# Bias of the last spatial sum on VectorE, one mask for all heads, and a new order table

## The chip, the cores and the metric

The kernel runs on one core of a Trainium2 chip. The metric is the device time of one execution in microseconds (us), the median over several runs. The engines are named as the profile names them: PE (TensorE matmuls, PEld its weight loads), DVE (VectorE), ACT (ScalarE), POOL (GpSimd) and SP (SyncE, which issues nearly all DMAs).

## The reference

Two layers stand one behind the other. The first is a gated recurrence over 768 steps for 4 batches and 8 heads of width 48; the second is a feed-forward block with a spatial sum over the sequence. Inputs and output are float32.

```python
# first layer, for each batch and head (D = 48), t = 0 .. 767
state = alpha[t, :, None] * state + outer(k[t], v[t])      # 48 x 48
y[t]  = q[t] @ state
# second layer: x is y with the heads side by side, [4, 768, 384]
h   = relu(x @ w_in)                                       # 384 -> 1024
u, v = h[..., :512], h[..., 512:]
v_n = (v - mean(v)) / sqrt(var(v) + 1e-6)                  # over the 512
v_s = einsum('ts,bsd->btd', w_spatial, v_n) + b_spatial[None, :, None]
out = (u * v_s) @ w_out                                    # 512 -> 384
```

## The kernel before

The sequence is cut into chunks of 128 steps, 6 for each batch and 24 in all. In a chunk the recurrence becomes matrix products: cumulated sums of log(alpha) (`cum`), keys and queries scaled by their exponentials (`kt`, `qt`), their transposes (`tr`, `trk`), scores (`sc`), a causal mask on the scores (`m`), and the output `y` from the masked scores and from the state of the chunk before. The first eight chunks are done in pairs with even and odd steps apart (`pair`, lines 368 to 584), the other sixteen one by one (`first`, lines 586 to 742).

The mask is a multiplication on DVE of a PSUM bank of scores (128 x 512: four heads of 128) with a bf16 tile of zeros and ones. The tiles are built once at the start: `mask4` (line 166, four equal triangles side by side, for single chunks, read on line 717) by POOL in `c_m4`, and `mask2` (line 184, for pairs, one set of four equal triangles for each of two parities, read on line 546) by two memsets on DVE (line 1031) and four selections on POOL (`c_m2`, line 230; the selections show as line 196).

In the second layer each batch has six groups of x @ w_in for v (`v`) and eight for u (`u`), eight spatial sums (`s`, one for each of four slices of 128 features and each half of the sequence), and six output tiles (`o`; the last tile of the last batch goes in two halves, `oh`). A spatial sum is six matmuls into one bank (line 780). For 31 of the 32 sums DVE then adds the bias `bsp_bc` into a float32 buffer `vsb` (line 928), and a second instruction on POOL or DVE multiplies with `uT` into `gT` (`g`, line 941). For the 32nd (`last`, line 907) the bias is put into the bank by a matmul of `ident` with `bsp_bc` ahead of the six, and one DVE instruction multiplies bank and `uT` into `gT` (line 921).

No scheduler runs on the chip or in the compiler. Each step is an `Op` with the engines that may do it; `replay` (line 62) walks through a table `PLAN` (line 58) that was worked out ahead, whose words give the engine and the number of a step. So the table sets the order on each engine, and for steps with a choice also the engine. Each engine works through its instructions in that order and waits at each for what it needs. PSUM has eight banks, taken in turn in the order in which the table starts steps. A word of the table can carry numbers behind colons: for each, `bank` (line 126) puts one float32 matmul on a constant tile `junk` of so many columns ahead of the step on PE (line 138). Nothing reads what these fillers make; they occupy PE near the start. One filler shows as two matmul records in the profile.

Of the kernel before, what the change touches and what calls it, by code (L numbers as in the profile page):

```python
# [9 lines left out]
FP32 = mybir.dt.float32  # L10
# [64 lines left out]
def kernel(  # L75
# [76 lines left out]
    def copy_pairs(eng, out, in_):  # L152

        copy(eng, *((out.bitcast(FP32), in_.bitcast(FP32)) if eng == "ACT" else (out, in_)))

    def relu(eng, out, in_):
        if eng == "ACT":
            nc.scalar.activation(out=out, in_=in_, func=AF.Relu)  # L158
        else:
            ENG[eng].tensor_scalar_max(out=out, in0=in_, scalar1=0.0)  # L160
# [24 lines left out]
    sbd_bufs = [consts.tile([128, HP, 2 * D], BF16, name=f"sbd{i}") for i in range(NB)]  # L185

    def zero_padding(t):

        flat = t.bitcast(FP32)
        nc.vector.memset(flat[:, :, :, D // 2:32], 0.0)  # L190
        if t.shape[2] > H:
            nc.vector.memset(flat[:, :, 0::3, 0:D // 2], 0.0)

    def triangle(t, pattern, base=0, step=1):

        nc.gpsimd.affine_select(
            out=t, in_=t, compare_op=ALU.is_gt, fill=1.0, base=base, channel_multiplier=step, pattern=pattern)
# [170 lines left out]
    def pair(j):  # L368
# [158 lines left out]
        for par in range(2):  # L527
            def sc(_, par=par):
                for s in range(2):
                    st[f"pt{s}{par}"] = bank([128, HP, 128])  # L530
                for hp in range(HP):
                    for s in range(2):
                        for ci in range(2):
                            rows = slice(64 - 64 * s, 64 - 64 * s + D)
                            nc.tensor.matmul(  # L535
                                out=st[f"pt{s}{par}"][halves(ci), hp, :], lhsT=st["kT"][rows, par, hp, halves(ci)],
                                rhs=q_cols(rows, hp, ci), start=True, stop=True)

            sls = [Slot(ring), Slot(ring)]
            op(("sc", j, par), "PE", 0.41, sc, got(("ev", "k", j, par), ("ev", "q", j, 0), ("ev", "q", j, 1)),  # L540
               prio=P + 7, take=sls, cols=768)
            for s in range(2):
                def mk(_, par=par, s=s):
                    if f"ptm{par}" not in st:
                        st[f"ptm{par}"] = work.tile([128, 2, HP, 128], BF16, name="ptm", bufs=4)
                    nc.vector.tensor_tensor(  # L546
                        out=st[f"ptm{par}"][:, s], in0=st[f"pt{s}{par}"], in1=mask2[:, par], op=ALU.mult)

                op(("m", j, par, s), "DVE", 0.6, mk,
                   got(("sc", j, par), ("y", 2 * j - 4), ("y", 2 * j - 3), ("c_m2", par)), prio=P + 7.5, use=[sls[s]])  # L550
# [35 lines left out]
    def first(i):  # L586
# [126 lines left out]
        def mk(s):  # L713
            def emit(_):
                if "ptm" not in st:
                    st["ptm"] = work.tile([128, 2, HP, 128], BF16, name="ptm", bufs=4)
                nc.vector.tensor_tensor(out=st["ptm"][:, s], in0=st[f"pt{s}"], in1=mask4, op=ALU.mult)  # L717
            return emit

        for s, sl in ((0, sl0), (1, sl1)):  # L720
            op(("m", i, s), "DVE", 0.6, mk(s), got(("sc", i), ("y", i - WK), ("c_m4",)), prio=P + 7.5, use=[sl])
# [184 lines left out]
    def second_s(b, dsl, th):  # L906
        last = b == B - 1 and dsl == NDS - 1 and th == 1
        mms = []
        if last:
            mms.append(mm(  # L910
                lambda ps: ps[:, 0:TH], lambda: ident, lambda: bsp_bc[:, th, :], True, False))
        for st in range(NT):
            mms.append(mm(
                lambda ps: ps[:, 0:TH].rearrange("p (c t) -> p c t", c=3), lambda st=st: bt[b]["vn"][:, st, dsl * 128:(dsl + 1) * 128],
                lambda st=st: w_spT[:, 3 * th:3 * th + 3, st, :], st == 0 and not last, st == NT - 1))
        hold = {}
        cols = slice(th * TH, (th + 1) * TH)

        def evac(eng, ps):
# [207 lines left out]
```

## Time and profile before

| what | value |
|---|---|
| median of 3 runs | 139.5 us (139.48 to 140.99) |
| the profiled execution | 139.22 us |
| its span, first to last instruction | 137.4 us |
| granted TensorE clock, mean | 0.995 |
| POOL busy | 92.9 us (68% of the span) |
| DMA | 28.64 MB, mean 208 GB/s |

The span is 1.8 us shorter than the time of the same execution. Rows of the profile that group instructions give, behind the bar, their busy time in us and the mean duration of one in ns, and behind a second bar the idle time of the engine just before them. Rows of the timeline and of the chain begin with the start in us from the span's start and the length in us; xN says how many instructions are merged in a row.

### The profile page before, as it was taken

The numbers are of one execution on the slowest core, as the hardware profiler recorded it, in microseconds if no ns is written. First come the engines' busy times: TensorE is split into PE (matmuls) and PEld (weight loads), VectorE is DVE, ScalarE is ACT, GpSimd is POOL, SyncE is SP. The second block draws the span as 40 slices with busy tenths as digits, with TensorE's granted clock in tenths as the row PEclk, the third lists the DMA queues.
The fourth block names the chain that finished last, engine by engine and source line by source line (L and its number), as shares of the span: only waits on it lengthen the run. The fifth ranks groups of instructions, "written<-read, shape, count | busy, mean of one in ns | idle before, by whom it ended". The sixth has DMA issues, their size and how long they took to land.

```text
span 137.4 us, 5023 instructions
## 1 busy us (share of the span) xinstructions
PE 132.7 (97%) x1943; PEld 88.4 (64%) x1943; DVE 116.1 (84%) x278; ACT 101.3 (74%) x286; POOL 92.9 (68%) x165
## 2 busy tenths in 40 slices
PE   6999999999999999999999999999999999999990
PEld 6768885757667655775667665656666666555660
DVE  7157989998998979998899999989999989878640
ACT  3488687999874799989974887999966757760241
POOL 4734998899894898793399999825666785202910
PEclk9999999999999999999999999999999999999998
DMA  3999999998979899899998989999994602940355
GB/s 95 319 322 328 275 343 328 331 293 243 319 120 314 160 193 203 166 208 193 207 210 160 212 168 199 196 200 212 193 183 114 169 10 108 350 171 6 130 188 197
DMA packets 89000, 28.64 MB, mean 208 GB/s; under 512 B 83728, under 2 KB 87440, under 8 KB 88976
## 3 DMA queue, kind: packets, MB, share of 16 engines
q1 hardware_dynamic: 88800, 28.22, 83.8%
q8 instruction: 15, 0.25, 0.7%
q10 hardware_dynamic: 144, 0.10, 0.2%
q14 instruction: 9, 0.07, 0.1%
q0 software_dynamic: 32, 0.00, 0.0%
HBM read 23.60 MB, written 4.72 MB: 206 GB/s over the span
## 4 chain that ended last, share of the span: by engine, by line
PE 95%; ACT 1%; issue 1%; DVE 0%; ACTq 0%
PE bank L780 58%; PE bank L138 7%; PE bank L671 3%; PE bank L706 3%; PE bank L470 3%; PE bank L734 2%; PE bank L618 2%; PE bank L692 2%; PE bank L535 2%; PE bank L728 2%; PE bank L406 2%; PE bank L343 2%; PE bank L505 2%; PE bank L562 1%; PE bank L320 1%; PE bank L792 1%
## 5 line engine op out<-in xcount | busy, mean ns | idle before, releaser
L780 PE MATMUL bank<-w_spT,vn 128*128 128x384 bf16 x192 | 35.1, 326 | 0.0
L941 POOL TENSOR_TENSOR gT<-vsb,uT 128x384 bf16<-128x384 f32 x25 | 22.8, 928 | 9.2 <-DVE vsb L928 8.6
L780 PEld LDWEIGHTS <-vn 128*128 128x128 bf16 x192 | 17.5, 97 | 10.5
L717 DVE TENSOR_TENSOR ptm<-bank,mask 128x512 bf16<-128x512 f32 x32 | 20.6, 681 | 0.1
L642 POOL TENSOR_TENSOR kt<-kc,binv 128x384 bf16<-128x384 f32 x15 | 13.9, 932 | 9.6 <-ACT binv L630 5.4
L780 PE MATMUL bank<-xT,w_in 128*128 128x384 bf16 x96 | 19.4, 326 | 0.0
L780 PE MATMUL bank<-w_in,xT 128*128 128x512 bf16 x72 | 19.2, 379 | 0.0
L928 DVE TENSOR_TENSOR vsb<-bank,bsp_bc 128x384 f32<-128x384 f32 x31 | 16.6, 552 | 2.0 <-PE bank L780 1.6
L780 PE MATMUL bank<-w_out_sb,gT 128*128 128x384 bf16 (+1 forms) x100 | 18.2, 319 | 0.0
L158 ACT ACTIVATE uT<-bank 128x384 bf16<-128x384 f32 x25 | 11.9, 495 | 5.5 <-PE bank L780 5.5
L150 POOL CAST sbd<-state 64x192 bf16<-64x192 f32 x40 | 13.7, 344 | 2.6 <-DVE state L290 0.5
L845 DVE BATCH_NORM_STATS2 stats<-v_sb 128x6 f32<-128x512 bf16 x20 | 13.7, 686 | 0.2
L148 ACT COPY kqT<-bank 128x256 f32<-128x256 f32 x35 | 11.8, 387 | 2.6 <-PE bank L671 1.7
L158 ACT ACTIVATE v_sb<-bank 128x512 bf16<-128x512 f32 x18 | 10.8, 598 | 3.1 <-PE bank L780 2.6
L290 POOL TENSOR_TENSOR state<-state,bc 128x192 f32<-128x192 f32 x17 | 9.5, 559 | 4.9 <-DVE state L283 2.6
L780 PEld LDWEIGHTS <-w_in 128*128 128x128 bf16 x96 | 8.7, 97 | 6.1
L138 PE MATMUL bank<-junk 128*128 128x64 f32 (+5 forms) x44 | 11.4, 389 | 1.1 <-DVE junk L1012 1.1
L780 PEld LDWEIGHTS <-gT 128*128 128x128 bf16 x100 | 8.9, 97 | 5.4 <-POOL gT L941 0.4
L148 ACT CAST x_sb<-bank 128x384 bf16<-128x384 f32 x20 | 9.4, 490 | 3.3 <-PE bank L734 2.3
L546 DVE TENSOR_TENSOR ptm<-bank,mask 128x512 bf16<-128x512 f32 x16 | 10.0, 682 | 0.5 <-PE bank L535 0.5
L612 ACT ACTIVATE la<-ac 128x384 bf16<-128x384 f32 x16 | 8.4, 533 | 2.5 <-DMA ac<-in_alpha_dram 2.5
L138 PEld LDWEIGHTS bank<-junk 128*128 128x128 f32 x44 | 8.8, 242 | 2.0 <-DVE junk L1012 1.1
(133 smaller groups left out, 290.7 us busy)
## 6 DMA issues: line engine op xcount, KB each, us to landing
ac<-in_alpha_dram SPq DMA_DIRECT2D x16, 192.0 KB, 4.6
kc<-in_k_dram SPq DMA_DIRECT2D x16, 192.0 KB, 4.0
qc<-in_q_dram SPq DMA_DIRECT2D x16, 192.0 KB, 3.9
vc<-in_v_dram SPq DMA_DIRECT2D x16, 192.0 KB, 3.9
raw_w<-in_moe_w_spatial_dram SPq DMA_DIRECT2D x3, 768.0 KB, 4.7
out_dram<-raw_w SPq DMA_DIRECT2D x11, 192.0 KB, 2.0
out_dram<-o_sb SPq DMA_DIRECT2D x9, 192.0 KB, 1.9
ac<-in_alpha_dram SPq DMA_DIRECT2D x4, 384.0 KB, 4.6
```

The source lines that it names most:

```text
L138: nc.tensor.matmul(out=flat[:, 0:cols].rearrange("p (a b) -> p a b", a=4), lhsT=junk, rhs=junk[:, None, 0:n].to_broadcast([128, 4, n]), st ...
L148: nc.scalar.copy(out=out, in_=in_)
L150: ENG[eng].tensor_copy(out=out, in_=in_)
L158: nc.scalar.activation(out=out, in_=in_, func=AF.Relu)
L290: ENG[eng].tensor_tensor(out=st["state"], in0=st["state"], in1=st["bc"][:, :, None].to_broadcast([128, HP, D]), op=ALU.mult)
L546: nc.vector.tensor_tensor(out=st[f"ptm{par}"][:, s], in0=st[f"pt{s}{par}"], in1=mask2[:, par], op=ALU.mult)
L642: ENG[eng].tensor_mul(out=k_blocks(kt3)[:, :, :, 0:D], in0=quad(st["kc"]), in1=st["binv"])
L717: nc.vector.tensor_tensor(out=st["ptm"][:, s], in0=st[f"pt{s}"], in1=mask4, op=ALU.mult)
L780: return lambda ps: nc.tensor.matmul(out=out(ps), lhsT=lhsT(), rhs=rhs(), start=start, stop=stop)
L845: nc.vector.bn_stats(out=stats, in_=d["v_sb"][:, tt, :])
L928: nc.vector.tensor_tensor(out=hold["vs"], in0=ps[:, 0:TH], in1=bsp_bc[:, th, :], op=ALU.add)
L941: ENG[eng].tensor_tensor(out=bt[b]["gT"][:, dsl, cols], in0=hold["vs"], in1=bt[b]["uT"][:, dsl, cols], op=ALU.mult)
```

## The change

Three things are changed. The 32nd spatial sum is treated as the 31 others are: the matmul with `ident` is gone, a bias addition and a separate multiplication come in place of the one multiplication. The masks hold one triangle (`ut_ones`, which was there already, in place of `mask4`) or one for each parity (`mask2`), and are read with a repeat over the heads; `mask4` and its step are gone, and `mask2` is built by one memset on DVE and two selections on POOL. And the table is a new one, since steps are numbered anew: nearly every engine's order is different, some steps go to another engine, and the fillers are others.

```diff
 PLAN = """
-S110 Q111 D0 D17 D5 G47 Q48 D3 D6 D1 S49 Q50 D11 D2 D15 S53 Q54 D13 D12 G14 D4 A118 S51 Q52 G16 A57 S55 Q56 P119:192:64:128:192:320:192:192:64 G9 P58
...
+S107 Q108 D2 D6 D0 D3 D1 D10 S46 Q47 D4 D14 D5 G15 D11 S48 Q49 D12 D7 G13 A115 S52 Q53 G8 P116:192:128:512:128:64 A54
...
-    mask4 = consts.tile([128, 4, 128], BF16, name="mask4")
...
-    mask2 = consts.tile([128, 2, 4, 128], BF16, name="mask2")
+    mask2 = consts.tile([128, 2, 128], BF16, name="mask2")
...
-    def c_m4(_):
-        nc.gpsimd.memset(mask4.bitcast(FP32), 0.0)
-        triangle(mask4, [[0, 4], [-1, 128]])
+    def of_heads(mask):
+
+        return mask[:, None, :].to_broadcast([128, HP, 128])
...
-    def c_m2(par):
-
-        def emit(_):
-            for ci in range(2):
-                triangle(mask2[64 * ci:64 * ci + 64, par], [[0, 4], [-1, 2], [-2, 64]], par, 2)
-        return emit
+    def c_m2(_):
+        for ci in range(2):
+            triangle(mask2[64 * ci:64 * ci + 64], [[1, 2], [-1, 2], [-2, 64]], 0, 2)
...
-                        out=st[f"ptm{par}"][:, s], in0=st[f"pt{s}{par}"], in1=mask2[:, par], op=ALU.mult)
+                        out=st[f"ptm{par}"][:, s], in0=st[f"pt{s}{par}"], in1=of_heads(mask2[:, par]), op=ALU.mult)
...
-                nc.vector.tensor_tensor(out=st["ptm"][:, s], in0=st[f"pt{s}"], in1=mask4, op=ALU.mult)
+                nc.vector.tensor_tensor(out=st["ptm"][:, s], in0=st[f"pt{s}"], in1=of_heads(ut_ones), op=ALU.mult)
...
     def second_s(b, dsl, th):
-        last = b == B - 1 and dsl == NDS - 1 and th == 1
+        last = False
...
-    op(("c_m4",), "POOL", 0.95, c_m4, prio=-8.0 if PAIRS else -18.0)
...
-        for par in range(2):
-            op(("c_mz", par), "DVE", 0.25, lambda _, par=par: nc.vector.memset(mask2[:, par].bitcast(FP32), 0.0), prio=-18.2)
-            op(("c_m2", par), "POOL", 1.4, c_m2(par), got(("c_mz", par)), prio=-18.0 + par)
+        op(("c_mz",), "DVE", 0.12, lambda _: nc.vector.memset(mask2.bitcast(FP32), 0.0), prio=-18.2)
+        op(("c_m2",), "POOL", 0.75, c_m2, got(("c_mz",)), prio=-18.0)
```

Three places show what the new table moves. The first is PE at the start of the program: the fillers (line 138 before, 188 after, matmuls of `junk`) and the first cumulated sums (line 406 before, 452 after). Before:

```order
L138 MATMUL bank0_85<-junk_97 128x192
L138 MATMUL bank0_85<-junk_97 128x64
L138 MATMUL bank0_85<-junk_97 128x128
L138 MATMUL bank0_85<-junk_97 128x192
L138 MATMUL bank0_85<-junk_97 128x320
L138 MATMUL bank0_85<-junk_97 128x192 x2
L138 MATMUL bank0_85<-junk_97 128x64
L406 LDWEIGHTS le_pair_116
L406 MATMUL bank0_85<-la1_108,le_pair_116 128x384
```

The same place after:

```order
L188 MATMUL bank0_85<-junk_96 128x192
L188 MATMUL bank0_85<-junk_96 128x128
L188 MATMUL bank0_85<-junk_96 128x512
L188 MATMUL bank0_85<-junk_96 128x128
L188 MATMUL bank0_85<-junk_96 128x64
L452 LDWEIGHTS le_pair_115
L452 MATMUL bank0_85<-la1_107,le_pair_115 128x384
```

Ahead of the first sum there are 1344 columns of fillers before and 1024 after. Over the whole program it is 3200 columns in 22 fillers before and 2368 in 15 after; all of them stand in the first quarter of PE's steps.

The second place is POOL near the start, where the masks were built (line 196 before; line 245 after, ahead of this piece), between the identity's copy and the products for the keys (`kt`, lines 442 and 488). Before:

```order
L1020 COPY ident_q_95<-ident_94 128x2x64
L203 MEMSET ut_ones_93 128x128
L196 AFFINE_SELECT ut_ones_93<-ut_ones_93 128x128
L442 TENSOR_TENSOR kt0_111<-kc_163,binvp1_114 128x4x2x48
L290 TENSOR_TENSOR state_303<-state_303,bc2_246 128x192
L196 AFFINE_SELECT mask2_118<-mask2_118 64x512 x2
L442 TENSOR_TENSOR kt1_112<-kc_203,binvp0_113 128x4x2x48
L150 CAST vbp_400<-vc_249 128x384
```

The same place after:

```order
L1066 COPY ident_q_95<-ident_94 128x2x64
L488 TENSOR_TENSOR kt1_111<-kc_211,binvp2_114 128x4x2x48
L488 TENSOR_TENSOR kt1_111<-kc_211,binvp0_112 128x4x2x48
L200 CAST sbd0_118<-state_284 64x4x48 x2
L336 TENSOR_TENSOR state_320<-state_320,bc2_217 128x192
L200 CAST vbp_397<-vc_269 128x384 x2
```

The two selections that stood ahead of the second pair's keys are gone from there, and POOL makes both of that pair's keys, where before DVE made one.

The third place is DVE at the end of the program: the last bias additions (`vsb`), multiplications (`gT`) and copies of output tiles (`raw_w`, `o_sb`). Before:

```order
L928 TENSOR_TENSOR vsb0_122<-bank3_88,bsp_bc_105 128x384
L928 TENSOR_TENSOR vsb1_123<-bank0_85,bsp_bc_105 128x384
L928 TENSOR_TENSOR vsb2_124<-bank2_87,bsp_bc_105 128x384
L921 TENSOR_TENSOR gT_2568<-bank3_88,uT_2565 128x384
L150 COPY raw_w_3143<-bank5_90 128x384
L150 COPY o_sb_3162<-bank0_85 128x384
```

The same place after:

```order
L974 TENSOR_TENSOR vsb1_122<-bank2_87,bsp_bc_104 128x384
L987 TENSOR_TENSOR gT_2567<-vsb0_121,uT_2564 128x384
L974 TENSOR_TENSOR vsb2_123<-bank1_86,bsp_bc_104 128x384
L974 TENSOR_TENSOR vsb3_124<-bank3_88,bsp_bc_104 128x384
L987 TENSOR_TENSOR gT_2567<-vsb3_124,uT_2564 128x384
L200 COPY raw_w_3125<-bank6_91 128x384
L200 COPY raw_w_3125<-bank0_85 128x384
L200 COPY raw_w_3125<-bank2_87 128x192
```

The last multiplication now reads a buffer that the instruction ahead of it fills, another one (`vsb0`) stands two places ahead, and DVE copies the last half tile, which ACT copied before. On PE three output tiles (twelve matmuls of 384 columns) stand between the last sum and the first matmul that needs the last multiplication; before it were two (eight matmuls).

More of the change, by code (lines that the diff above doesn't have):

```diff
@@ new lines @@
+A91 D201 P203:128 A208 A95 G140 D190 A134 P205 P96 G189 D142 P92 P194 A97 D206 S21 Q22 P148 D93 A195 G141 P192 A204
+D150 A193 G20 A18 D149 P212 P215 G19 D213 P264 G143 S326 Q327 A265 P101 D217 G144 D216 P151 A102 G202 S26 Q27 P152
+D214 A191 P156 P98 S324 Q325 A153 D103 A330 P207 P218 A157 D209 D210 A99 P154 P158 P219 D155 G211 P341 D100 A220 P160
+A159 G23 A342 P221 P223 G24 D161 P343 A222 P331 A224 D25 P171 A344 D162 S30 Q31 A353 A104 P225 P163 S328 Q329 D346
+A226 A332 P167 D106 A164 P350 D172 A333 P227 S383 Q384 A168 G29 D335 P230 A351 S385 Q386 D173 A228 G28 P169 A231 D229
@@ new lines @@
+P402 A436 A367 P409 G437 A438 P372 P290 D410 A373 S593 Q594 G277 P368 D296 P377 A369 D439 A40 S496 Q497 G43 P374 D403
+A378 D41 G42 D297 P441 P411 G269 P282 A413 A442 D412 D379 P291 A375 S500 Q501 P414 A443 G404 D292 A470 S466 Q467 P283
+D376 P448 S498 Q499 A601 P471 D284 P298 A473 D449 G285 A504 S464 Q465 P421 D415 A472 P505 G440 P306 D450 S502 Q503
+A506 G293 A475 P286 D416 A508 S468 Q469 P423 G405 A422 D476 P287 A299 D509 G507 S599 Q600 A424 P419 A307 D288 P451
+S597 Q598 D420 G474 P444 A452 P417 D445 D446 S595 Q596 P453 P511 D418 A454 P478 A513 P302 D479 A480 G477 A455 D512
@@ new lines @@
+G289 P485 A303 P514 D486 A380 P481 S664 Q665 P456 G447 A510 D482 D515 P310 S633 Q634 G483 A457 D487 G484 P602 A608
+P314 S627 Q628 D516 A603 A604 A311 P488 G605 A606 P517 S710 Q711 D489 P318 A518 D607 S629 Q630 A315 P490 D458 P519
+P609 A491 A492 P612 A611 S706 Q707 G642 P493 D520 A459 D521 G382 D319 P535 A494 D610 S666 Q667 P522 D381 A495 G460
+D613 S668 Q669 P616 D536 A523 P533 D461 A524 G614 D617 P531 A635 P541 D525 A672 S670 Q671 P545 D618 A526 P673 P549
+S631 Q632 A714 D527 D528 P636 A534 D615 P529 S708 Q709 A637 P542 A675 A674 P619 A677 D543 P546 G676 S712 Q713 A532
@@ new lines @@
+D678 P550 A530 S744 Q745 G639 D547 A638 P561 A620 D551 A640 P715 P562 S748 Q749 G544 A716 D641 P621 A717 A719 P680
+D622 P643 G718 D563 S778 Q779 A682 P553 A679 D720 P646 A623 G564 A645 S782 Q783 P554 D681 D644 P687 D555 G548 P722
+S746 Q747 A752 P650 D647 A724 P537 D688 A721 G648 P565 A723 D651 G552 P683 P538 D689 S780 Q781 G649 P566 D684 D652
+P557 G685 S750 Q751 P690 D567 P653 D539 A691 S874 Q875 P558 A654 D568 G540 P753 A786 D559 P692 S878 Q879 P655 A754
+P729 D657 P624 A693 D730 A755 A757 G686 S945 Q946 A656 P577 D758 G756 D694 S784 Q785 P725 D731 P787 P658 A788 D578
@@ new lines @@
+A790 P732 D726 G789 A625 P569 D791 A733 D659 S880 Q881 G556 P760 A570 P734 P793 D761 A762 P695 S908 Q909 G727 A794
+D735 D626 A795 G560 A882 P698 S876 Q877 A736 D660 A696 P767 G728 P796 A697 P883 D769 S987 Q988 P737 G759 A699 D768
+P581 S910 Q911 A889 D797 A661 P704 S914 Q915 A884 D798 P763 P573 A885 A582 D764 A887 D662 P770 S989 Q990 G765 A738
+D888 P585 G886 A705 D771 S1028 Q1029 P589 A739 D792 G766 A574 D586 P772 P890 A773 D590 P702 A916 S587 Q588 G663 D892
+A774 P893 S912 Q913 P799 D891 P775 D740 A800 S993 Q994 A703 D894 P801 P897 A741 D802 G895 P700 S991 Q992 A803 D743
@@ L59 @@
+S1140 Q1141 P1146 D1143 S1152 Q1153 P1154 S1144 Q1145 A1147 D1155 S1148 Q1149 A1156 Q1157
 """
```

29 lines of the change are left out of this document (26 added, 3 removed).

## The prediction

> **What bounds the kernel now.** I read the page's head first, then the chain that ended last, then busy times over the long middle, then who waits.
>
> ```profile
> span 137.4 us, 5023 instructions
> PE 95%; ACT 1%; issue 1%; DVE 0%; ACTq 0%
> PEclk9999999999999999999999999999999999999998
> 1.05 5.17 PE bank L138 x16
> 116.64 17.18 PE bank L780 x105
> 134.22 0.32 ACT raw_w L148
> 17.50:121.50 104.00, 103.86 (x1620) 67.11 (x1615) 96.99 (x228) 85.97 (x251) 77.69 (x134) 1.00 0.89 207
> PE bank L138 <- DVE junk L1012: 1.1, 1, 1.1
> PE bank L423 <- ACT binvp L414: 0.2, 1, 0.2
> ```
>
> The chain is PE from the fillers' start at 1.05 to 133.8 (116.64 + 17.18); only a pause, the last copy and the last store follow. PE's granted clock, the row of nines, is full. The long row is a stretch of 104 us from the first chunks' outputs to the last batch's sums, with busy times of PE, PEld, DVE, ACT and POOL in turn: PE 103.86, DVE 96.99, so DVE is idle 104.00 - 96.99 = 7.0 us. The two last rows are all the waits of PE that the profile shows. PE takes its instructions in order and hardly stops, so the time is what stands in PE's row, plus the waits that the new order makes. Matmul records overlap, so a wait shorter than a matmul's own drain does not show.
>
> **The fillers.** Those at the very start first.
>
> ```profile
> 4.25 0.84 ACT L397 ACTIVATE la<-ac 128x768 bf16<-128x768 f32 x1 [2.23 <-DMA ac<-in_alpha_dram]
> 5.53 0.84 ACT L397 ACTIVATE la<-ac 128x768 bf16<-128x768 f32 x1 [0.44 <-DMA ac<-in_alpha_dram]
> 6.01 0.53 PE L406 MATMUL bank<-la,le_pair 128*128 128x384 bf16 x1
> 6.33 0.39 PE L406 MATMUL bank<-la,lt_pair 128*128 128x384 bf16 x1
> 6.56 0.33 PE L406 MATMUL bank<-la,le_pair 128*128 128x384 bf16 x1
> 6.72 0.33 PE L406 MATMUL bank<-la,lt_pair 128*128 128x384 bf16 x1
> 7.38 0.59 PE L138 MATMUL bank<-junk 128*128 128x256 f32 x2
> 7.81 0.49 PE L406 MATMUL bank<-la,le_pair 128*128 128x384 bf16 x2
> ```
>
> 1344 columns took 6.01 - 1.05 = 4.96 us, 3.69 ns a column. The 1024 columns after take 3.8 us; `junk` is now filled behind three other memsets, and even if that costs half a microsecond they end near 5.4 instead of 6.01. But the second logarithm ends at 5.53 + 0.84 = 6.37, released by a DMA that SP still issues second, and the sums that read it started at 6.56. PE waits there as before. This part is worth 0.
>
> Behind that point there were 3200 - 1344 = 1856 columns and are 2368 - 1024 = 1344. A filler of 256 columns held PE from 7.38 to 7.81, 0.43 us or 1.68 ns a column. 512 columns fewer are 0.86 us. That counts only if what follows a filler is ready earlier too. I take the whole 0.86, since two things ahead of it get shorter. One is POOL:
>
> ```profile
> 12.74 1.39 POOL L196 TENSOR_SCALAR_AFFINE_SELECT mask<-mask 64x512 bf16<-64x512 bf16 x2
> 14.21 0.92 POOL L442 TENSOR_TENSOR kt<-kc,binvp 128x384 bf16<-128x384 f32 x1
> ```
>
> Mask building held the second pair's keys for 1.39 us, and now stands in the first microseconds, where POOL waits anyway. The other is that keys, queries and values of the first pair are loaded in the order in which they are used. If neither helps, the 0.86 comes back as waits: the ends are -0.86 and 0.
>
> **The last sum.**
>
> ```profile
> 125.26 0.55 DVE L941 TENSOR_TENSOR gT<-vsb,uT 128x384 bf16<-128x384 f32 x1
> 126.43 4.72 POOL L941 TENSOR_TENSOR gT<-vsb,uT 128x384 bf16<-128x384 f32 x5 [8.60 <-DVE vsb L928]
> 126.68 1.08 DVE L941 TENSOR_TENSOR gT<-vsb,uT 128x384 bf16<-128x384 f32 x1
> 128.93 0.33 PE L780 MATMUL bank<-bsp_bc,ident 128*128 128x384 bf16 x1
> 129.09 1.14 PE L780 MATMUL bank<-w_spT,vn 128*128 128x384 bf16 x6
> 130.07 4.07 PE L780 MATMUL bank<-w_out_sb,gT 128*128 128x384 bf16 x28
> 130.34 0.56 DVE L921 TENSOR_TENSOR gT<-bank,uT 128x384 bf16<-128x384 f32 x1 [0.58 <-PE bank L780]
> ```
>
> The matmul with `ident` held PE for 129.09 - 128.93 = 0.16 us, which goes: -0.16. In its place DVE does two instructions. The sums' last matmul ends at 129.09 + 1.14 = 130.23, DVE starts 0.11 later; addition and multiplication are 0.56 + 0.55, so `gT` is there about 1.2 us after the sum. PE has twelve matmuls ahead of the first that needs it, each 0.163 us after the other (six from 129.09 to 130.07), 1.95 us from 0.16 before the sum's end: the cover is 1.79 us. With POOL multiplying at the same time, though, such a DVE instruction took 1.08 (at 126.68) instead of 0.55 (at 125.26). Then it is 1.75 us, which just fits; had DVE also to make good a delay of 0.5 from the multiplication two places ahead, PE would wait 0.5. Term 0, bounds 0 and +0.5.
>
> [...]
>
> The last half tile is copied by DVE instead of ACT, and ACT issues its store all the same; both began right behind PE, so 0.
>
> **The masks with a repeat.** The trace has no mask read so. The nearest rows are the state's product, which reads one operand with a repeat, and its sum, which doesn't.
>
> ```profile
> L290 DVE TENSOR_TENSOR state<-state,bc x3: 348/408/605, 80.3 to 113.0; 128x192 f32<-128x192 f32 x3
> L285 DVE TENSOR_TENSOR state<-bank,state 128x192 f32<-128x192 f32 x16 | 5.6, 351 | 0.4 <-POOL state L290 0.3
> L717 DVE TENSOR_TENSOR ptm<-bank,mask 128x512 bf16<-128x512 f32 x32 | 20.6, 681 | 0.1
> ```
>
> 348 ns at best with a repeat, 351 without. Between 0 and 408 - 351 = 57 ns for each of 48 products (32 here, 16 for pairs) is 0 to 2.7 us of DVE time. A saving is excluded, since as many elements pass. I take 0: the slower two of the three stood beside POOL, and the fastest is the operation by itself.
>
> **What moves onto DVE.** Counted engine by engine, 274 instructions of DVE in the table's order become 289; ACT loses eight, POOL thirteen.
>
> ```profile
> L160 DVE TENSOR_SCALAR uT<-bank 128x384 bf16<-128x384 f32 x7 | 3.7, 545 | 0.4 <-PE bank L780 0.4
> L160 DVE TENSOR_SCALAR v_sb<-bank 128x512 bf16<-128x512 f32 x2 | 1.3, 658 | 0.0
> L877 DVE TENSOR_SCALAR vn<-v_sb,mvs,rstd 128x512 bf16<-128x512 bf16 x15 | 5.9, 421 | 1.8 <-ACT rstd L870 1.8
> L150 DVE COPY raw_w<-bank 128x384 f32<-128x384 f32 x5 | 2.8, 551 | 0.7 <-PE bank L780 0.7
> L150 DVE CAST vb<-vc 128x384 bf16<-128x384 f32 x1 | 0.4, 390 | 0.0
> DVE xT L150 <- PE bank L343: 1.3, 2, 0.8
> DVE vn L877 <- ACT rstd L870: 1.2, 3, 0.6
> DVE w_spT L150 <- ACT rstd L869: 0.4, 1, 0.4
> DVE state L285 <- POOL state L290: 0.3, 1, 0.3
> ```
>
> Five `uT` more are 2.7 us, three `v_sb` 2.0, three `vn` 1.3, two `gT` 1.1; five copies of outputs fewer are -2.75; the bias addition and the lost multiplication cancel. The smaller ones (six casts, three other copies net, a memset and a key product fewer) I put at seven times 0.39, 2.7. Together 7 us. By where they stand, some 4 of them fall into the 104 us, against 7.0 us of idle DVE. The last four rows, of that stretch alone, show what ended the idle time: 1.2 + 0.4 + 0.3 = 1.9 us were waits for ACT and POOL, which stay; the rest was waiting for PE or was nothing, and may be filled. 7.0 - 4 = 3.0 is over 1.9, so on the average DVE still keeps up with PE. It will not at each place, as eight banks is all that stands between them. I charge a tenth of the 4 us, +0.4; the ends are 0 and 4.
>
> **The sum.** 139.22 (the profiled execution: 137.4 of span and 1.8 around it) - 0.86 - 0.16 + 0.4 = 138.6 us. The median shown is 0.28 higher than that execution, so the forecast for a median is 138.9 us, with a range of its own from 137.9 (no charge for DVE) to 139.8 (no gain from the fillers, 0.4 at the end).
>
> **The rivals.** One: the fillers only covered waits, and PE waits in their place. For it speaks that early PE follows ACT and DVE (the wait on `binvp`); against it, the 1.39 us that POOL gets back. Time 138.9 + 0.86 = 139.8 with DVE's charge, 139.3 without.
>
> Two, on the other side: DVE becomes the bound of the middle. The place is the 104 us between the first outputs and the last sums, the price is what DVE takes on there, 4 us, and it decides when DVE's idle time in that stretch falls under the 1.9 us that others make it wait: then PE waits for banks to be read. For it: DVE is at 93% (96.99 of 104) already; the mask's upper bound of 2.7 us would be enough. Against it: ACT and POOL are relieved, so their 1.9 may shrink. Time 139.5 - 1.02 + 4 + 0.4 = 142.9 us.
>
> Three: the clock. The sums that began at 6.01 and 6.33 were 0.32 apart, those at 6.56 and 6.72 only 0.16, so PE ran at half speed until about 6.4, 5.4 us after its first matmul, although the granted clock reads full there. The fillers now start later and are fewer. Should the half speed last past 6.4 through the next 768 columns of fillers and four sums, that is 768 x 2.0 ns + 4 x 0.16 = 2.2 us: 141.1. Against it: PE still has hardly a pause there. [...]
>
> Four: the new order also removes waits that hide between overlapping matmuls.
>
> ```profile
> L343 PEld LDWEIGHTS <-x_sb 64*128 64x128 bf16 x96 | 2.3, 95 | 2.0 <-ACT x_sb L148 1.4 <-issue 0.3 <-ACT vb L148 0.3
> L706 PEld LDWEIGHTS <-kqT 48*128 48x128 bf16 x128 | 3.7, 94 | 1.6 <-issue 0.4 <-ACT v_sb L831 0.4 <-ACT vn L841 0.3
> ```
>
> Weight loads waited 2.0 and 1.6 us, most of it for ACT, which now does less. All of it gone would give 138.9 - 3.6 = 135.3. Against it: most of this idle time lies beside busy matmuls.
>
> **Chances.** The forecast 0.42, rival one 0.14, two 0.28, three 0.04, four 0.12. About 2% (2.8 us: under 136.7, over 142.3) is what a measurement of this kernel can tell from no change. Most of rival four (0.10, where over 2.2 of its 3.6 us come) lies under it, and six tenths of rival two over it: faster 0.10, same 0.73, slower 0.17. The range from 136.9 to 142.9 us leaves out nearly all of rival four and, beyond rival two's own time, a third of it.
>
> **What would show it.** In the changed profile the row of waits should name PE nowhere over 0.3 us; fillers should take about 2.3 us behind the first sums; the 48 mask products should stay at 0.68 us; DVE's idle time in the stretch should be near 3 us. Waits of PE on DVE, or mask products of 0.74 us, would mean rival two. A matmul of half tiles that waits for `gT` at the end would cost the 0.5. A first score matmul that comes no earlier than before would mean rival one.

## The result, and the profile after

| what | before | after |
|---|---|---|
| median of 20 runs each | 139.98 us | 141.39 us |
| the profiled execution, its span | 139.22 us, 137.4 us | 141.61 us, 139.8 us |
| second measurement of both (26 and 12 runs) | 139.32 us | 140.29 us |
| a second profiled execution of the changed kernel, its span | | 139.54 us, 137.8 us |

The changed kernel is slower, by 0.5 to 0.7%: its time is 1.0071 of the kernel before, 95% interval 1.0042 to 1.0100, and in the second measurement 1.0050, interval 1.0021 to 1.0079. The ratios leave disturbed runs out, so they are not those of the medians. The forecast, 138.9 against a median of 139.5, was 0.996. Of the changed kernel there are two profiles, one of a long execution and one of a short one, and the first thing to read is how they differ. First, of the long one, the chain that ended last and the waits of PE.

```profile
PE 60%; SPq 10%; ACT 7%; DMA 7%; POOL 6%; DVE 5%; issue 4%; POOLq 0%; DVEq 0%
PE bank L188 <- DVE junk L1058: 1.7, 1, 1.7
PE bank L826 <- DVE ptm L763: 0.9, 1, 0.9
PE bank L581 <- ACT kqT L198: 0.5, 1, 0.5
PE bank L717 <- DVE xT L200: 0.4, 1, 0.4
PE bank L516 <- ACT bc L557: 0.4, 1, 0.4
PE bank L717 <- POOL kt L688: 0.2, 1, 0.2
PE bank L664 <- DVE ptm L763: 0.2, 1, 0.2
```

Before, PE made up 95% of the chain; now 60%, and SP's queue and DMA together 17%. PE waits in six places besides the start. The short execution of the same kernel has another chain, and the waits on `ptm`, `xT` and `kt` are gone from it:

```profile
PE 83%; SPq 4%; ACT 4%; DMA 4%; issue 2%; POOL 1%; DVE 1%; POOLq 0%
PE bank L188 <- DVE junk L1058: 1.7, 1, 1.7
PE bank L581 <- ACT kqT L198: 0.5, 1, 0.5
PE bank L516 <- ACT bc L557: 0.4, 1, 0.4
PE bank L664 <- ACT la L658: 0.2, 1, 0.2
```

So the two waits at the start (`kqT`, `bc`) are in both executions; the three longest in the middle are in one only. What they are is seen in the longest, at 43.58 us. The profile puts it down to DVE's `ptm`. Below are rows of the timeline: SP's issue of a load of v, two steps of ACT (with one more between them) and the matmuls of a spatial sum on PE, first of the long execution, then of the short one.

```profile
35.55 3.15 SPq L644 DMA_DIRECT2D vc<-in_v_dram  x1
42.38 0.51 ACT L198 CAST vb<-vc 128x384 bf16<-128x384 f32 x1 [1.00 <-DMA vc<-in_v_dram]
...
43.23 0.30 ACT L198 COPY w_spT<-bank 128x192 f32<-128x192 f32 x1
43.58 0.65 PE L826 MATMUL bank<-w_spT,vn 128*128 128x384 bf16 x3 [0.85 <-DVE ptm L763]
```

```profile
35.59 2.42 SPq L644 DMA_DIRECT2D vc<-in_v_dram  x1
41.16 0.52 ACT L198 CAST vb<-vc 128x384 bf16<-128x384 f32 x1
...
42.03 0.32 ACT L198 COPY w_spT<-bank 128x192 f32<-128x192 f32 x1
42.52 0.66 PE L826 MATMUL bank<-w_spT,vn 128*128 128x384 bf16 x3
42.73 1.28 DVE L763 TENSOR_TENSOR ptm<-bank,ut_ones 128x512 bf16<-128x512 f32 x2
```

In the short execution PE begins at 42.52, ahead of DVE's `ptm` at 42.73, so these matmuls never needed `ptm`: the row names what ended at the same moment. They need `w_spT`, which ACT copied until 42.03 + 0.32 = 42.35 there and until 43.23 + 0.30 = 43.53 in the long one. And ACT was late because the cast of `vb` stood ahead of that copy and waited 1.00 us for its load. In the kernel before, ACT has the two steps the other way round:

```profile
41.14 0.59 ACT L148 COPY w_spT<-bank 128x192 f32<-128x192 f32 x2
41.56 0.57 ACT L148 CAST vb<-vc 128x384 bf16<-128x384 f32 x1
```

In that order a late load of v cannot hold up the weights. The other two waits of the long execution are read alike. POOL's product for the keys (`kt`) and the transposes on PE that read it:

```profile
54.96 1.79 POOL L688 TENSOR_TENSOR kt<-kc,binv 128x384 bf16<-128x384 f32 x2 [0.42 <-DMA kc<-in_k_dram]
56.81 0.29 PE L717 MATMUL bank<-ident,kt 64*128 64x64 bf16 x8 [0.24 <-POOL kt L688]
110.42 0.91 POOL L688 TENSOR_TENSOR kt<-kc,binv 128x384 bf16<-128x384 f32 x1 [1.30 <-DMA kc<-in_k_dram]
111.09 0.26 DVE L200 COPY xT<-bank 128x192 bf16<-128x192 bf16 x1
111.39 0.29 PE L717 MATMUL bank<-ident,kt 64*128 64x64 bf16 x8 [0.41 <-DVE xT L200]
```

The products end at 54.96 + 1.79 = 56.75 and 110.42 + 0.91 = 111.33, each 0.06 ahead of PE's start, and each waited for a load of k. (At 111 us a copy of DVE ends at 111.35, 0.02 later than the product, and the row names that one.) The three waits come to 0.85 + 0.24 + 0.41 = 1.5 of the 2.0 us between the two executions.

They account for the long execution alone. Three other kernels below keep the new order behind the sixth chunk, and their profiles have no wait of PE behind such a load, yet their executions took 140.02 (`new_no_fill`), 140.46 (`old_start_new_rest`) and 140.75 us (`new_relieved`), longer than the short one. In the second of them, for instance, ACT casts `vb` at 41.61 without waiting and has copied `w_spT` by 42.47 + 0.32 = 42.79.

The rest of the profile answers to the forecast's terms. PE's fillers and the first scores, then the first group of v, in the long execution:

```profile
1.68 3.89 PE L188 MATMUL bank<-junk 128*128 128x192 f32 x10 [1.68 <-DVE junk L1058]
12.92 0.69 PE L581 MATMUL bank<-kqT 48*64 48x128 bf16 x16
21.64 0.61 PE L826 MATMUL bank<-w_in,xT 128*128 128x512 bf16 x2
```

In the profile before, the same two are these:

```profile
13.43 1.03 PE L535 MATMUL bank<-kqT 48*64 48x128 bf16 x48
21.33 0.82 PE L780 MATMUL bank<-w_in,xT 128*128 128x512 bf16 x3
```

The first scores come 0.5 us earlier, the first group of v 0.3 later: the start gains nothing that lasts. In the short execution the start is the same to some hundredths. POOL's keys of the second pair, two waits of PE, and the first group of v:

```profile
11.61 1.90 POOL L488 TENSOR_TENSOR kt<-kc,binvp 128x384 bf16<-128x384 f32 x2 [4.42 <-DMA kc<-in_k_dram]
18.55 0.38 PE L516 MATMUL bank<-ident,qt 128*128 128x128 bf16 x4 [0.36 <-ACT bc L557]
20.79 0.64 PE L581 MATMUL bank<-kqT 48*64 48x128 bf16 x32 [0.46 <-ACT kqT L198]
21.63 0.60 PE L826 MATMUL bank<-w_in,xT 128*128 128x512 bf16 x2
```

POOL has nothing left to build here, but waits 4.42 us for a load of k. In both profiles of the changed kernel the chain up to 12.5 us is SP's issues, this load (6.57 to 11.46) and POOL's product, and not PE; in the kernel before it begins with PE's fillers.

The masks' products in the long execution, and the end (PE's output tiles, the last multiplication on DVE) in the short one:

```profile
L763 DVE TENSOR_TENSOR ptm<-bank,ut_ones 128x512 bf16<-128x512 f32 x32 | 20.4, 679 | 0.3 <-PE bank L752 0.2
L592 DVE TENSOR_TENSOR ptm<-bank,mask 128x512 bf16<-128x512 f32 x16 | 10.0, 681 | 1.1 <-PE bank L581 1.1
130.38 4.07 PE L826 MATMUL bank<-w_out_sb,gT 128*128 128x384 bf16 x28
131.24 1.01 DVE L987 TENSOR_TENSOR gT<-vsb,uT 128x384 bf16<-128x384 f32 x1
```

A product takes 679 and 681 ns (681 and 682 before), and the end's matmuls take 4.07 us, as before, although the last multiplication took 1.01. They begin 130.38 - 130.07 = 0.3 later than before: the short execution is as far behind at the end as at the first group of v.

### The profile page after: what moved, and what is told of

Read it like the earlier page. It is cut to its first block, busy times and chain, and to the rows that moved or that the text cites. A ratio compares the mean times of both kernels' runs of the same rounds, so it can differ in the third digit from the quotient of the medians.

```text
span 139.8 us, 4965 instructions
## 1 busy us (share of the span) xinstructions
PE 130.9 (94%) x1917; PEld 84.5 (60%) x1928; DVE 122.0 (87%) x294; ACT 99.1 (71%) x278; POOL 85.5 (61%) x150
## 4 chain that ended last, share of the span: by engine, by line
PE 60%; SPq 10%; ACT 7%; DMA 7%; POOL 6%; DVE 5%; issue 4%; POOLq 0%; DVEq 0%
PE bank L826 40%; DMA kc<-in_k_dram 7%; SPq L644 6%; SPq L432 4%; PE bank L752 2%; PE bank L717 2%; POOL kt L688 2%; PE bank L780 2%; PE bank L738 2%; PE bank L581 2%; PE bank L664 2%; PE bank L774 1%; ACT uT L208 1%; ACT bank L482 1%; PE bank L389 1%
## 5 line engine op out<-in xcount | busy, mean ns | idle before, releaser
L826 PE MATMUL bank<-w_spT,vn 128*128 128x384 bf16 x192 | 36.1, 326 | 0.9 <-DVE ptm L763 0.9
L763 DVE TENSOR_TENSOR ptm<-bank,ut_ones 128x512 bf16<-128x512 f32 x32 | 20.4, 679 | 0.3 <-PE bank L752 0.2
L826 PE MATMUL bank<-w_in,xT 128*128 128x512 bf16 x61 | 17.2, 379 | 0.6
L198 ACT COPY kqT<-bank 128x256 f32<-128x256 f32 x35 | 12.5, 381 | 4.5 <-DVE gT L987 1.8
L336 POOL TENSOR_TENSOR state<-state,bc 128x192 f32<-128x192 f32 x17 | 8.7, 514 | 5.3 <-DVE state L331 3.0
L592 DVE TENSOR_TENSOR ptm<-bank,mask 128x512 bf16<-128x512 f32 x16 | 10.0, 681 | 1.1 <-PE bank L581 1.1
L208 ACT ACTIVATE v_sb<-bank 128x512 bf16<-128x512 f32 x15 | 8.9, 603 | 1.5 <-PE bank L826 1.2
L208 ACT ACTIVATE uT<-bank 128x384 bf16<-128x384 f32 x20 | 9.6, 495 | 0.5 <-PE bank L826 0.5
L676 ACT ACTIVATE binv<-bank 128x384 bf16<-128x384 f32 x16 | 7.8, 489 | 2.9 <-PE bank L664 1.6
L188 PE MATMUL bank<-junk 128*128 128x128 f32 (+4 forms) x30 | 8.0, 399 | 1.7 <-DVE junk L1058 1.7
L698 DVE TENSOR_TENSOR qt<-qc,bank 128x384 bf16<-128x384 f32 x16 | 8.7, 548 | 0.6 <-ACT bank L693 0.3
```

Of the source, the lines that this page charges most:

```text
L198: nc.scalar.copy(out=out, in_=in_)
L336: ENG[eng].tensor_tensor(out=st["state"], in0=st["state"], in1=st["bc"][:, :, None].to_broadcast([128, HP, D]), op=ALU.mult)
L592: nc.vector.tensor_tensor(out=st[f"ptm{par}"][:, s], in0=st[f"pt{s}{par}"], in1=of_heads(mask2[:, par]), op=ALU.mult)
L698: nc.vector.tensor_mul(out=qt[:, :, ::-1, 0:D], in0=quad(st["qc"]), in1=st["cv"])
L826: return lambda ps: nc.tensor.matmul(out=out(ps), lhsT=lhsT(), rhs=rhs(), start=start, stop=stop)
```

## The experiments

Every kernel was timed against the kernel before in the same session; ratios are to that, with the 95% interval. Line numbers shift by a few from kernel to kernel. All of them compute the whole reference.

### Do the fillers hold PE back?

The changed kernel without the 1344 columns behind its first sum, and the kernel before without its 1856. The words of the table that change, the changed kernel's first:

```diff
-... P65:128 ... P72:64:256:128:192 ... P76:128 ... P124:64 ... P87:192 ... P186:64 ... P203:128
+... P65 ... P72 ... P76 ... P124 ... P87 ... P186 ... P203
...
-... P68:64 ... P129:256 ... P66:384 ... P64:64 ... P247:64
+... P68 ... P129 ... P66 ... P64 ... P247
```

> The changed kernel with no fillers behind the first cumulated sum (1344 columns fewer, the 1024 ahead of that sum kept). Theory 'fillers cover waits': the time is that of the changed kernel, ratio to the kernel before 1.003 to 1.011, with PE's waits in the first 25 us longer by about the 2.3 us of the fillers. Rival 'fillers are on the path', which my prediction took: 1 to 2 us less, ratio 0.993 to 1.000. A third outcome, over 1.015, would say that the fillers keep PE's clock up.

> The kernel before without the 1856 columns of fillers behind the first sum (those ahead of it kept). If these hold PE back, as the forecast had it, 1856 x 1.68 ns = 3.1 us fewer: 0.978. If they only cover waits, as the changed kernel without them showed (1.0073 against 1.0071 with them), 0.998 to 1.003.

Measured 1.0073 (1.0041 to 1.0104), where the changed kernel with them has 1.0071, and 1.0018 (0.9993 to 1.0042). Taking away 1856 x 1.68 ns = 3.1 us of PE's work gains nothing. Where it went, the waits of PE in the kernel before without fillers show:

```profile
PE bank L476 <- ACT binvp L467: 0.8, 1, 0.8
PE bank L459 <- ACT la L450: 0.6, 2, 0.3
```

Before, the first of these was 0.2 and the second did not show. The fillers stand where PE would wait, for ACT in these two rows and for DVE and POOL in others of 0.2 to 0.3.

### The steps or the table?

The three changed steps in the old order, and the table cut in two behind the output of the sixth chunk: old start with the new rest, and the reverse. The first line of the table tells them apart.

```diff
 PLAN = """
-S107 Q108 D2 D6 D0 D3 D1 D10 S46 Q47 D4 D14 D5 G15 D11 S48 Q49 D12 D7 G13 A115 S52 Q53 G8 P116:192:128:512:128:64 A54
...
+S107 Q108 D0 D5 G44 Q45 D3 D6 D1 S46 Q47 D10 D2 D14 S50 Q51 D12 D11 G13 D4 A115 S48 Q49 G15 A54 S52 Q53
...
```

> The changed steps (one triangle for all heads; the 32nd sum with a bias addition and a multiplication on VectorE) in the order of the kernel before, fillers included. Theory 'order': the steps alone are worth about -0.2 us (the 0.16 us matmul gone, mask products still 0.68 us), ratio 0.997 to 1.001. Rival 'steps': the repeat over heads or the longer end costs what was measured, ratio 1.005 to 1.010, with mask products of 0.70 us or more or a wait of PE at the last output tiles.

> The changed steps, in the old order up to the output of the sixth chunk (25 us), in the new one from there. Theory 'middle' (the new order's waits at 42, 56 and 110 us cost the time): ratio 1.005 to 1.010, the wait of about 1 us for a mask product near 42 us is still there. Rival 'start' (the first 25 us lose it): ratio 0.997 to 1.002.

> The complement: the changed steps, in the new order up to the output of the sixth chunk, in the old one from there. Theory 'middle': ratio 0.998 to 1.003, no wait of PE over 0.5 us after 25 us. Rival 'start': ratio 1.004 to 1.010.

> All three changed steps in the old order once more, beside which the masks alone measured 1.0017 and the last sum alone 1.0006. If these add up, 1.001 to 1.004 here, and the 1.0076 of the first time held too few runs; if the two together cost more than their sum, 1.006 to 1.010 again.

Old order throughout: 1.0076 (1.0048 to 1.0105) over six executions, and 1.0035 (1.0008 to 1.0063) over twelve when it was measured once more. Old start with new rest: 1.0095 (1.0070 to 1.0121). New start with old rest: 1.0029 (1.0003 to 1.0055). Beside the new start the new rest looks dearer than the old one (1.0071 and 1.0050 against 1.0029), but the intervals overlap; and the steps in the old order seemed to cost something as well, which had to be settled first.

### What in the steps costs?

Each part alone in the old order, both with the buffers at their old addresses, and the last sum left as it was behind a new start.

```diff
-    mask2 = consts.tile([128, 2, 4, 128], BF16, name="mask2")
+    mask2 = consts.tile([128, 2, 128], BF16, name="mask2")
...
-        last = b == B - 1 and dsl == NDS - 1 and th == 1
+        last = False
...
+    consts.tile([128, 4, 128], BF16, name="pad4")
-    mask2 = consts.tile([128, 2, 128], BF16, name="mask2")
+    mask2 = consts.tile([128, 2, 4, 128], BF16, name="mask2")[:, :, 0]
...
```

> The kernel before with the new masks alone (one triangle, read with a repeat), its order and its last sum kept. All three changed steps together in the old order had measured 1.0076 of the kernel before. Theory 'last sum': masks cost nothing, 0.998 to 1.002 here. Theory 'masks': the masks (their building, or what the smaller tiles move in SBUF) carry it, 1.004 to 1.010 here. Mask products 0.68 us in both.

> The kernel before with the new last sum alone (bias and multiplication by two DVE instructions), its order and its masks kept; in that order two output tiles stand between the sum and the first matmul that needs it. Theory 'last sum': 1.004 to 1.010, with PE waiting 0.5 us or more for the last multiplication near the end. Theory 'masks': 1.000 to 1.003, the 0.2 us of PE's wait that the run of all three steps showed there.

> All three changed steps in the old order, with 2.5 KB a partition of unused memory put back where the masks shrank, so that every later buffer lies at its old address. Theory 'address': 1.000 to 1.003, against 1.0076 without the memory. Theory 'steps': unchanged, 1.006 to 1.010.

> New masks, the new order up to the sixth chunk's output, the old order behind it, and the old last sum (bias by a matmul with the identity). The same with the new last sum measured 1.0029. If the last sum costs what PE waited at the end (0.2 us), 1.001 to 1.002; if it costs more, at or under 1.000; if the rest of the cost is in the masks, unchanged at 1.003.

Masks alone 1.0017 (0.9999 to 1.0035), last sum alone 1.0006 (0.9980 to 1.0032), old addresses 1.0013 (0.9992 to 1.0034), old last sum behind the new start 1.0010 (0.9979 to 1.0041). By the intervals none of these is told from its neighbour. The traces say more. The masks' kernel has a stop of DVE ahead of the state's sum; here with PE's matmuls that read the state:

```profile
25.03 0.36 DVE L334 TENSOR_TENSOR state<-bank,state 128x192 f32<-128x192 f32 x1 [0.44 <-issue]
26.82 0.33 PE L624 MATMUL bank<-sbd,kqT 128*128 128x96 bf16 x4 [0.17 <-POOL sbd L203]
```

The kernel before at the same place:

```profile
24.68 0.36 DVE L285 TENSOR_TENSOR state<-bank,state 128x192 f32<-128x192 f32 x1
26.55 0.33 PE L575 MATMUL bank<-sbd,kqT 128*128 128x96 bf16 x4
```

DVE stands still for 0.44 us with nothing that the profile shows to wait for ("issue"), and PE's matmuls come 0.27 later. A stop of 0.43 to 0.50 us ahead of this sum is in the profiles of all five measurements so far with the new masks and the old start (with the old addresses too), and not in those with the new start or with the last sum alone. Four of the five rows name nothing; that of `old_order_again` names the matmuls that the sum reads. But those end 0.52 to 0.54 us before the sum in all five, and 0.11 before it in the kernel before, so it is the same stop.

### What makes DVE stop?

Reading with a repeat from the old masks; POOL's building of the old single mask put back, unread; one memset of DVE put back, unread; and the same memset with all changed steps.

```diff
-                nc.vector.tensor_tensor(out=st["ptm"][:, s], in0=st[f"pt{s}"], in1=mask4, op=ALU.mult)
+                nc.vector.tensor_tensor(out=st["ptm"][:, s], in0=st[f"pt{s}"], in1=mask4[:, 0][:, None, :].to_broadcast([128, HP, 128]), op=ALU.mult)
...
+    op(("c_m4",), "POOL", 0.95, c_m4, prio=-8.0)
...
+        op(("c_mx",), "DVE", 0.25, lambda _: nc.vector.memset(spare.bitcast(FP32), 0.0), prio=-18.2)
```

> The kernel before with only the reading of the masks changed: the four triangles are built as before, and the products read the first of them with a repeat. Theory 'building': the repeat costs nothing, 0.998 to 1.002, DVE's sum of the state near 25 us starts at once, and PE reaches the state's matmuls at 26.5 us. Rival 'reading': DVE stops for 0.44 us ahead of that sum, as with the masks alone, and the time is 1.002 to 1.004.

> The new masks alone in the old order, but POOL still builds the old mask for single chunks at its old place (24 us), where nothing reads it. Theory 'two instructions of POOL': with them back, the stop of DVE near 25 us is gone, 0.999 to 1.002. Rival: the stop of 0.44 us stays, 1.001 to 1.004, and it comes from something else that the masks changed (one memset less on DVE, two selections less on POOL near 13 us).

> The new masks alone in the old order, with one more memset on DVE at the place where the old one stood (it fills a tile that nothing reads), so that DVE has as many instructions ahead of the state's sum near 25 us as in the kernel before; POOL's three dropped selections stay dropped. Theory 'place in DVE's stream': the stop of 0.44 us is gone and the time is 0.998 to 1.002. Rival 'POOL': the stop stays, 1.001 to 1.004, since what POOL no longer does near 13 us brings it about.

> All changed steps, the new masks and the new last sum, in the old order, with the one spare memset on DVE. Without the memset this measured 1.0076 and 1.0035. Theory 'stream': the steps themselves are free, 0.997 to 1.002, no stop of DVE near 25 us, and what the changed kernel lost (1.005 and 1.007) is the new table's. Rival: 1.003 to 1.007, the last sum costs as well in that order (PE's wait of 0.2 us near the end and more).

Reading alone: 1.0004 (0.9979 to 1.0029), no stop. POOL's building put back: 1.0035 (1.0009 to 1.0062), and the stop stays (0.48, put down to POOL's mask, which the sum does not read). The memset put back: 0.9980 (0.9957 to 1.0003), and the stop is gone:

```profile
24.68 0.36 DVE L335 TENSOR_TENSOR state<-bank,state 128x192 f32<-128x192 f32 x1
```

All changed steps with it: 1.0013 (0.9990 to 1.0036), no stop. So one useless instruction more on DVE, over 20 us earlier, takes the stop away. It goes with the place of the sum in DVE's stream of instructions (in this order it is there when 49 instructions of DVE stand ahead of the sum, and not when 50 do), not with what the masks are; why DVE stops there is not shown. The changed kernel, whose order is another, has no row of DVE with "issue" at all. In the old order the steps measured 1.0076 and 1.0035 with the stop and 1.0013 without it. So its loss is most likely its table's and not the steps'; that the steps cost as little in the new order is argued from the missing stop, not measured. No kernel tried beats the kernel before by more than its interval; the nearest is the one with the new masks and the memset.

### DVE's load, or the loads from memory?

The changed kernel again; the changed kernel with eight steps given back from DVE to ACT, and the kernel before with the same eight moved to DVE; and the changed kernel with its loads in the old sequence.

```diff
-... D254 D255 ... D980 ... D982 ... D986 ... D1085 ... D1093 ... D1095
+... A254 A255 ... A980 ... A982 ... A986 ... A1085 ... A1093 ... A1095
...
-... A257 A258 ... A983 ... A985 ... A989 ... A1088 ... A1096 ... A1098
+... D257 D258 ... D983 ... D985 ... D989 ... D1088 ... D1096 ... D1098
```

> The changed kernel once more, unaltered, for a second profile beside the runs that follow: 1.004 to 1.010 of the kernel before. In its first profile PE waited 1.0 us at 42.5 us for two copies and two mask products of DVE, 0.6 near 111 us for DVE, 0.4 near 56 us for POOL. Theory 'DVE': waits of PE for DVE at these or other places again, about 1 us in all, come what may of the single place. Rival 'chance': the long wait is gone, and the median is within 0.3% of the kernel before.

> The changed kernel with eight steps given back from DVE to ACT, where the kernel before had them: two copies of the turned spatial weights near 41 us, five evacuations of u and one of v of the last batch; the order of the steps is untouched. It takes 4.1 us of work off DVE (2 x 0.35 + 5 x 0.54 + 0.68). Theory 'DVE': the time falls towards the kernel before, 1.000 to 1.004, and the waits at 42 and 111 us shrink. Rival 'order': unchanged, 1.006 to 1.010, since the waits come from where steps stand and not from how much DVE does.

> The kernel before with the same eight steps moved from ACT to DVE, order untouched: 4.1 us more of DVE work. Theory 'DVE': slower by 0.4 to 1.5 us, 1.003 to 1.011, with new waits of PE for DVE. Rival 'order': under 1.003, for DVE has 7 us of idle time in the middle.

> The changed kernel with its loads issued in the kernel before's sequence, as early as the places of loads in the new table allow; everything else as in the changed kernel, which measured 1.005 and 1.007. Theory 'loads': late transfers cost part of it, 1.000 to 1.004. Rival 'engines': the sequence of loads is no matter, or steps now wait for loads that suited the other order, 1.005 to 1.012.

The changed kernel again: 1.0050 (1.0021 to 1.0079). The single wait at 43 us is gone, and with it all waits for DVE; but the median is still 0.97 us higher (140.29 against 139.32), so neither theory holds as written. The profiled execution was the shortest of its twelve, which range from 139.54 to 140.79.

Eight steps off DVE: 1.0104 (1.0066 to 1.0142), slower than the changed kernel by the medians (141.03 against 140.29, though the intervals overlap), with new waits of PE for ACT. Eight steps onto DVE in the old order: 1.0119 (1.0071 to 1.0166), that is 141.18 - 139.32 = 1.86 us for 4.1 us of work. A row of waits of the former, then one of the latter:

```profile
PE bank L829 <- ACT kqT L201: 0.3, 1, 0.3
```

```profile
PE bank L833 <- DVE o_sb L203: 0.6, 1, 0.6
```

Moving the same eight steps made it worse either way, clearly so in the old table. That each table's order is fitted to its share of the engines would explain it, but is not shown. "DVE has too much to do" does not explain the changed kernel.

The loads in the old sequence: 1.0711 (1.0652 to 1.0769). This is far outside what either theory expected. PE waits 3.1 us for `w_spT` at one place:

```profile
PE bank L829 <- ACT w_spT L201: 3.1, 1, 3.1
```

It shows how much hangs on the sequence of loads, but not that the new sequence is the worse one, since the old one is fitted to the old steps.

## Why the prediction was wrong

**What bounds the kernel.** PE, in its order: right for all but the start, and still so in the short execution (83% of the chain). Up to 12.5 us the chain of the changed kernel follows a load of k instead. That the time is PE's row plus the waits that the new order makes was right too. The waits were not found.

**The fillers.** "Worth 0" for those at the start held: they end 1.68 + 3.89 = 5.57 us, and the first scores are not held up by them. For those behind, the step "I take the whole 0.86, since two things ahead of it get shorter" failed. POOL no longer builds masks there and the first scores are 0.5 earlier, but POOL's keys now wait 4.42 us for a load, PE then waits 0.4 and 0.5 for `bc` and `kqT`, and the first group of v is 0.3 later, with the same work of PE ahead of it but for the fillers. The term was -0.86 and measured +0.3. Rival one had it: the fillers covered waits (its times, 139.3 and 139.8, still fell short of the medians). Its sign in the profile, a first score that comes no earlier, was put too early in the program; the first group of v was the place to look.

**The last sum.** The term 0 held: 4.07 us at the end in both, and the part alone measured 1.0006. Of the -0.16 for the matmul with `ident` no gain can be told (the part alone: 0.9980 to 1.0032). The 0.4 at the end that the forecast's range counts in, and by its sum rival two's time too, no run shows: in both profiles of the changed kernel PE has no wait there, and in the old order, with two output tiles ahead in place of three, the end's matmuls took 4.25 us with the last sum alone, 0.18 more.

**The masks.** The reading with a repeat is free: 1.0004, and 679 to 681 ns against 681 and 682, so the value taken from the fastest row was the right end of 0 to 2.7 us. That a dropped memset might cost something was nowhere in the forecast. In the changed kernel's own order the stop does not show.

**DVE.** It takes on 122.0 - 116.1 = 5.9 us by the two pages (7 were forecast), and 99.12 - 96.99 = 2.1 of them, not 4, in the stretch of 104 us. In the stretch from 17.5 to 121.5 us it is busy 99.12 us in the short execution:

```profile
17.50:121.50 104.00, 102.26 (x1594) 65.17 (x1603) 99.12 (x235) 83.61 (x245) 73.34 (x122) 1.00 0.86 201
```

(PE's sum here is short by some records of 512 columns that the trace lacks.) 104.00 - 99.12 = 4.9 us idle, over the 1.9 from which rival two was to decide, and no wait of PE for DVE: rival two did not come about. Nor does anything in this profile stand for the charge of +0.4. As a price of DVE work a tenth is too little outside a table made for it: there 4.1 us cost 1.86, nearly half (1.0 to 2.3 by the interval).

**What was missing.** Put the measured +0.3 at the first group of v in place of all terms, and the profiled execution comes to 139.22 + 0.3 = 139.5 us; the short one took 139.54. Behind that place gains and losses cancel. Leaving the 0.86 out of the forecast's sum gives 139.5 as well, but by luck: it keeps -0.16 and +0.4, neither of which any run shows as time. Nor is this the whole loss. The short execution is the shortest of its twelve; the shortest of the kernel before in that session took 138.86, and the medians lie 0.97 apart.

No term and no rival spoke of the loads, though DMA is busy 0.89 of the long stretch in the row of before that the forecast quoted. Of the 2 us of the long execution over the short one, 1.5 are shown to be loads: ACT and POOL do their steps in the order of the table, loads come up to 1.3 us late, and the new table has what PE needs next standing behind a step that waits for a load. The 0.8 us between the short execution and the median stay open. The three other profiles with the new order in the middle, 140.02 to 140.75 us, have no such wait of PE, so late loads are not shown to be the usual cause; and the experiment meant to test the loads changed too much at once.

## What to carry to other kernels

When a new order is judged, look at each step that waits for a load on an engine that goes in the table's order (ACT's cast waited 1.00 us here, and PE 0.85 behind it) and ask what stands behind it, and for whom; the profile of one execution shows only the loads that were late that time. Filler work that can be taken out without a gain (1856 columns here, for 1.0018) was covering a wait, so fewer fillers are no term of a sum until what follows them is shown to come earlier, some stages on. An engine that has less to do ahead of a load may only wait longer for that load, as POOL did here (4.42 us). A wait's row names what ended last: where two things ended within some hundredths of a microsecond (0.02 here, at 111 us), compare a second execution to see which of them was needed.

## What the runs showed of the hardware that was not expected

**A stop at a place in the stream.** DVE's stop of 0.44 us comes and goes with one instruction more or less ahead of it: it is there with the masks alone, and not with the spare memset. The page counts the packets that carry instructions in a run; in the kernel before:

```profile
q8 instruction: 15, 0.25, 0.7%
q14 instruction: 9, 0.07, 0.1%
```

These are 15 packets of 16 KB and 9 of 8 KB. The first of the 8 KB packets in the program starts at 24.80 us in the kernel before, 0.12 after the sum at 24.68, and at 24.29 in the long execution of the changed kernel, 0.38 ahead of the sum at 24.67. Neither has the stop. Which engine a packet is for, the trace does not say, and that the stop has to do with these packets is not shown.

**What it costs PE to change between whole and smaller matmuls.** In the kernel before, a matmul of 384 columns over all 128 rows and columns starts 162 ns ahead of the next such one, and 258 ns ahead of one over 64 or 48 rows (medians behind 17.5 us): some 96 ns for the change. There are 60 such changes, either way, before and 64 after. If each costs as much, the new order adds some 0.4 us, an estimate; the forecast had no term for it.

**When PE gets to its full pace.** In the profile of the kernel before, the first two sums were 0.32 us apart (6.01 and 6.33), at half the pace of later ones (0.16, at 6.56 and 6.72). In the kernel with the masks alone, whose fillers are the same, they are 0.16 apart and come 0.6 us earlier:

```profile
5.42 0.33 PE L455 MATMUL bank<-la,le_pair 128*128 128x384 bf16 x1
5.58 0.33 PE L455 MATMUL bank<-la,lt_pair 128*128 128x384 bf16 x1
```

So the sums stood 0.16 apart from 5.42 us on there and from 6.56 on in the kernel before, both with a first matmul at 1.05. Of the 0.6 us gained, 0.4 was lost again at once, in a wait for the second logarithm. Each of the two is one execution, so it is not shown whether the kernel or the execution makes the difference.

**One program, two executions.** The two profiles of the changed kernel differ by 2.0 us in the same instructions, 1.5 of it by when loads land.
